# Column sums of the attention weights by GpSimd and a two-part bf16 product, with a new order of all steps

## The chip, the cores and the metric

The kernel runs on one core of a Trainium2 chip. The core has TensorE for matrix products (PE in the profile; PEld are its weight loads), VectorE (DVE), ScalarE (ACT) and GpSimd (POOL) for elementwise work, and SyncE (SP), whose queue issues DMA transfers here, as GpSimd's queue does too. The metric is the device time of one execution in microseconds (us). Three runs of the kernel before took 220.65, 221.41 and 221.46 us, the median is 221.41.

## The reference

Eight batches of eight heads, 512 tokens of 64 features and 32 state rows per head. Attention goes both ways between tokens and state; the result, 544 rows of 512 features per batch, goes through a layer of 2048 features with a periodic activation.

```
scores  = scale * x @ state.T          a  = softmax(scores)     xread = a @ state
scores2 = scale * state @ x.T          a2 = softmax(scores2)    sread = a2 @ x
y = concatenate([xread, sread], axis=tokens)        # heads side by side: 512 features
h = y @ w_in
g = h + sin(alpha * h)**2 / (alpha + 1e-9)
out = g @ w_out
```

Both softmaxes use the same exponentials E (tokens by state): `a` divides them by their sums over the state rows, `a2` by their sums over the tokens, which are the column sums of E.

## The kernel before, in words

The whole program is a list of steps by name, `ORDER`. The kernel walks through it; each step calls a method of `Steps`, and nothing is rescheduled: every engine executes its instructions in the order of the list and waits only for what it reads, for what it overwrites, and for a free buffer. A step's suffixes are its batch and tile numbers, the engine (A, V or G) and, where it opens one, a PSUM bank. There are eight banks of one tile each, so a step that opens a bank waits until the tile that held it has been read.

For a batch b the steps are:

- `lx` loads x (GpSimd's queue, cast to bf16), `pk` packs it by token, `td` transposes it by DMA (SyncE's queue). Batch 0 comes in by `lq`, `xq`, `xtq`, `xc` instead, and batch 1 is transposed on TensorE by `xt`, `xc`.
- `sc` makes the scores, `ex` the exponentials E (two groups of four heads), `rs` and `rr` their row sums and reciprocals (VectorE), `nm` the normalized A (GpSimd), `ad` its DMA transpose AT (SyncE's queue; `at`, `ac` for batch 0).
- `m` makes M, state times w_in, one slab of 512 columns at a time for both groups: eight matmuls of 64 x 32 tiles, that run side by side. `me` copies a slab out of PSUM, one group at a time. w_in arrives in four slices (`li`), one per slab, w_out in four (`lo`), one per four feature tiles, both from GpSimd's queue.
- `h` makes one feature tile of 128 columns for the 512 tokens, AT and M multiplied and summed over two groups (`hg` is one group's half of it). `si` is the sine (ScalarE), `sq` its square (on A, V or G by the suffix), `gt` puts g together on VectorE. The bank of h is read by `si` and by `gt`.
- `o` multiplies gT of a feature tile with w_out and adds it to one of four blocks of 128 tokens; `oc` copies a finished block out of PSUM and `os` stores it from SyncE's queue. There are six buffers for finished blocks.
- `w` multiplies E with x over four token blocks (16 matmuls of 64 columns), `cs` makes the column sums, `rc` their reciprocals, `xs` the normalized state rows. All eight batches' state rows go through the layer together as a ninth block, t = 8 (four products of 256 columns per feature tile).
- `warm_up` multiplies a tile of zeros, into a bank that nobody reads.

`cs` as it was: for each of four token blocks and each of two head parities r, ones (128 x 64) times 128 columns of E, into the upper or the lower half of the partitions; eight matmuls per batch, each on half of the array's columns.

Of the kernel before, what the change touches and what calls it, by code (L numbers as in the profile page):

```python
# [10 lines left out]
ALU = mybir.AluOpType  # L11
# [22 lines left out]
me.1.1.1.A warm_up.2.128.2 gt.0.2 si.0.0 warm_up.2.128.2 warm_up.2.128.6 warm_up.2.128.3
warm_up.2.128.2 warm_up.2.128.6 me.0.1.0.A gt.0.1 sq.0.0.G m.0.2.3.2 si.0.3 m.1.2.5.6 hg.0.4.0.7
me.0.2.0.V me.0.2.1.A hg.0.4.1 sq.0.3.G hg.0.6.0.4 me.1.2.1.V hg.0.6.1 si.0.4 hg.0.7.0.3 hg.0.11.0.2
me.1.2.0.V si.0.6 hg.0.7.1 sq.0.4.G hg.0.5.0.6 gt.0.0 hg.0.5.1 si.0.7 hg.0.11.1 hg.0.8.0.5 hg.0.8.1
sq.0.6.A gt.0.3 sq.0.7.G o.0.3.0.2.0 si.0.5 gt.0.4 o.0.3.2.3 o.0.0.0.2.1 si.0.11 o.0.0.2.3 gt.0.6
sq.0.5.G o.0.0.3.4 o.0.2.0.1.7 si.0.8 o.0.3.3.5 sq.0.11.A gt.0.7 hg.0.9.0.4 sq.0.8.G o.0.2.1.2
gt.0.5 o.0.2.2.4 hg.0.9.1 gt.0.11 o.0.0.4.5 hg.0.10.0.3 si.0.9 o.0.2.4.5 gt.0.8 o.0.0.5.6 o.0.3.5.6  # L40
sq.0.9.A o.0.3.6.8 pk.1.0.V hg.0.10.1 xt.1.1.6 pk.1.1.V si.0.10 gt.0.9 xt.1.0.2 xc.1.1.0.A sq.0.10.G
o.0.2.5.6 xc.1.1.1.V xc.1.0.0.A o.0.0.6.7 xc.1.0.1.V o.0.0.7.8 o.0.2.6.7 sc.1.1.5 gt.0.10 sc.1.0.4
m.0.3.6.2 ex.1.0 o.0.2.7.8 me.0.3.0.V o.0.1.0.3.3 me.0.3.1.V o.0.1.3.6 hg.0.13.0.6 o.0.1.6.7 ex.1.1
rs.1.0 hg.0.13.1 m.1.3.2.4 si.0.13 o.0.1.7.8 rr.1.0 rs.1.1 nm.1.0.0.4.G o.0.1.8.9 hg.0.12.0.5
o.0.3.8.9 rr.1.1 hg.0.12.1 me.1.3.0.V o.0.0.8.9 nm.1.1.0.4.G o.0.1.9.10 o.0.0.9.10 me.1.3.1.V
si.0.12 o.0.0.10.11 o.0.3.9.11 sq.0.13.G ad.1 hg.0.15.0.2 sq.0.12.A o.0.1.10.12 hg.0.15.1 gt.0.12
o.0.2.8.10 si.0.15 o.0.2.10.11 gt.0.13 o.0.0.11.12 hg.0.14.0.4 sq.0.15.A hg.0.14.1 o.0.3.11.13
si.0.14 gt.0.15 o.0.0.12.13 o.0.1.12.13 o.0.3.13.14 sq.0.14.A pk.2.0.V o.0.1.13.14 pk.2.1.V h.1.2.5
gt.0.14 h.1.4.6 td.2 si.1.2 lx.3.0.1 h.1.0.2 si.1.4 o.0.0.13.15 sq.1.2.V h.1.1.4 si.1.0 gt.1.2
sq.1.4.G o.0.3.14.16 si.1.1 o.0.2.11.13 sq.1.0.A oc.0.3.V h.1.6.5 sq.1.1.G gt.1.4 o.0.2.13.14 os.0.3  # L50
h.1.3.0 si.1.6 gt.1.0 o.0.1.14.16 si.1.3 sq.1.6.G h.1.13.6 gt.1.1 oc.0.1.A o.0.2.14.15 o.0.0.15.16
si.1.13 h.1.15.2 sq.1.3.G lx.4.0.1 gt.1.6 os.0.1 o.0.2.15.16 oc.0.0.A h.1.5.4 sq.1.13.V oc.0.2.V
si.1.15 h.1.7.3 os.0.0 gt.1.3 o.1.1.0.1.5 si.1.5 os.0.2 h.1.8.1 sq.1.15.G gt.1.13 o.1.1.1.2 si.1.7
o.1.2.0.2.7 sq.1.5.A o.1.1.2.3 sq.1.7.G h.1.12.0 gt.1.15 si.1.8 h.1.9.6 gt.1.5 o.1.2.2.3 si.1.12
sq.1.8.G o.1.2.3.5 gt.1.7 si.1.9 o.1.1.3.4 h.1.10.2 sq.1.12.A pk.3.1.V h.1.11.4 sq.1.9.G gt.1.8
o.1.2.5.6 si.1.10 o.1.2.6.7 gt.1.12 h.1.14.3 si.1.11 sq.1.10.G o.1.2.7.8 gt.1.9 sc.2.1.1 si.1.14
o.1.1.4.7 sq.1.11.A pk.3.0.V sq.1.14.G o.1.1.7.8 gt.1.10 td.3 o.1.2.8.9 sc.2.0.0 o.1.1.8.9 gt.1.11
o.1.1.9.10 ex.2.0 o.1.3.0.2.6 gt.1.14 o.1.3.2.4 o.1.2.9.10 o.1.3.4.5 o.1.2.10.12 ex.2.1 o.1.2.12.13
rs.2.0 o.1.1.10.11 m.2.2.2.4.3.0 rr.2.0 rs.2.1 o.1.2.13.14 nm.2.0.0.4.G me.2.3.0.A o.1.2.14.15 w.0.1
rr.2.1 me.2.2.1.A me.2.3.1.V o.1.3.5.6 nm.2.1.0.4.G me.2.2.0.A o.1.3.6.7 o.1.2.15.16 cs.0 oc.1.2.A  # L60
m.2.0.3.4.0.2 ad.2 rc.0 o.1.3.7.8 me.2.1.1.A o.1.3.8.9 sc.3.0.7 xs.0.1 me.2.1.0.A o.1.1.11.12 os.1.2
me.2.0.0.V sc.3.1.2 me.2.0.1.A o.1.1.12.13 o.1.3.9.10 xs.0.0 pk.4.1.V pk.4.0.V td.4 o.1.3.10.11
ex.3.0 o.1.1.13.16 ex.3.1 rs.3.0 o.1.3.11.13 oc.1.1.A o.1.3.13.14 rr.3.0 h.2.0.0 rs.3.1 nm.3.0.0.4.G
os.1.1 o.1.3.14.16 si.2.0 rr.3.1 h.2.1.3 oc.1.3.V nm.3.1.0.4.G h.2.2.4 h.2.8.1 os.1.3 h.2.3.7 ad.3
si.2.2 o.1.0.0.3.2 si.2.8 sq.2.0.V o.1.0.3.4 sq.2.2.G gt.2.0 h.2.4.5 si.2.1 o.1.0.4.6 si.2.3
sq.2.8.G o.1.0.6.7 gt.2.2 h.2.9.6 si.2.4 o.2.3.0.1.0 o.1.0.7.8 sq.2.1.G o.1.0.8.9 sq.2.3.A gt.2.8
o.1.0.9.10 h.2.5.4 si.2.9 gt.2.3 o.1.0.10.11 sq.2.4.G o.1.0.11.12 si.2.5 h.2.7.1 gt.2.1 o.1.0.12.13
sq.2.9.A sq.2.5.G o.1.0.13.14 gt.2.4 o.1.0.14.15 si.2.7 o.1.0.15.16 o.2.0.0.1.7 gt.2.9 o.2.0.1.2
oc.1.0.A h.2.6.3 sq.2.7.G gt.2.5 o.2.3.1.2 os.1.0 o.2.3.2.3 si.2.6 h.2.10.5 o.2.3.3.4 sq.2.6.A
# [88 lines left out]
class Steps:  # L158
# [505 lines left out]
```

## Time and profile before

| what | value |
|---|---|
| median of three runs | 221.41 us |
| the profiled execution | 221.22 us |
| its span, first to last instruction | 219.2 us |
| granted TensorE clock | 1.00 |
| VectorE: gT (L576) | 96.8 us in 144 |
| VectorE: squares (L201) | 7.0 us in 16 |
| ScalarE: Sin (L560) | 88.8 us in 144 |
| ScalarE: squares (L569) | 31.4 us in 53 |
| GpSimd: squares (L201) | 75.9 us in 75 |
| GpSimd: A (L201) | 16.6 us in 16 |

"Busy" is the time in which an engine executes; overlapping instructions count once. For each group of instructions the profile shows the line, the engine, the tiles written and read, the number, the busy time, the mean duration of one and the idle time ahead of them with what ended it. A matmul's duration includes the time that its result takes to come out, which overlaps with the next one; the chain of waits shows the distance from one to the next, so costs on TensorE are read from it. "issue" is time for which the profile shows no wait.

### The profile page before, as it was taken

How to read it: one execution, taken by the hardware profiler on the slowest of the kernel's cores; microseconds unless marked ns; L12 is line 12 of the kernel's file. 1: busy time of each engine (PE TensorE's matmuls, PEld its weight loads, DVE VectorE, ACT ScalarE, POOL GpSimd, SP SyncE). 2: the span in 40 equal slices, each digit the busy share in tenths (PEclk: the TensorE clock that was granted, in tenths of full speed). 3: DMA queues.
4: the chain of work that ended last, by engine and by line, in shares of the span. 5: the costliest groups of instructions: out<-in, count | busy, mean ns of one | idle time of the engine just before them, and what ended most of it. 6: DMA issues, size and time to landing. Idle time of an engine off the chain costs nothing.

```text
span 219.2 us, 4303 instructions
## 1 busy us (share of the span) xinstructions
PE 211.4 (96%) x1593; PEld 104.5 (48%) x1619; DVE 162.9 (74%) x287; ACT 173.4 (79%) x297; POOL 106.2 (48%) x114
## 2 busy tenths in 40 slices
PE   7989999999999999999999999999999999999994
PEld 3744544444444534444454444454445555665452
DVE  3769996999787789989888788888667987661201
ACT  4799778997998979898996999798848896785111
POOL 5959533895195647753943387273501082121000
PEclk9999999999999999999999999999999999999999
DMA  6999999987491029167145327470220211012042
GB/s 195 178 206 204 205 204 146 217 169 133 101 238 48 3 92 143 57 144 96 48 79 131 109 71 96 134 110 0 48 100 0 98 48 48 0 51 96 1 143 96
DMA packets 38052, 23.48 MB, mean 107 GB/s; under 512 B 20992, under 2 KB 33680, under 8 KB 38032
## 3 DMA queue, kind: packets, MB, share of 16 engines
q1 hardware_dynamic: 26128, 15.08, 26.5%
q0 software_dynamic: 11648, 8.13, 26.0%
q8 instruction: 12, 0.20, 0.3%
q14 instruction: 8, 0.07, 0.1%
q10 hardware_dynamic: 256, 0.01, 0.1%
HBM read 17.44 MB, written 8.91 MB: 120 GB/s over the span
## 4 chain that ended last, share of the span: by engine, by line
PE 90%; DMA 6%; POOL 1%; issue 1%; ACT 0%
PE o_ps L587 54%; PE h_ps L537 22%; DMA w_in_sb<-in_moe_w_in_dram 5%; PE m_ps L488 4%; PE h_ps L543 3%; PE h_ps L552 2%; PE w_ps L450 2%; PE s_ps L399 2%; PE w_ps L461 1%; DMA s<-in_state_dram 1%; POOL w_in_sb L282 1%; PE x_ps L376 0%; POOL st_nat L267 0%; POOL s01b L255 0%; ACT o_sb L595 0%
## 5 line engine op out<-in xcount | busy, mean ns | idle before, releaser
L587 PE MATMUL o_ps<-w_out_sb,gT 128*128 128x512 bf16 (+2 forms) x542 | 133.9, 373 | 1.6 <-issue 1.0
L576 DVE SCALAR_TENSOR_TENSOR gT<-s,inva_sb,h_ps 128x512 bf16<-128x512 bf16 (+1 forms) x144 | 96.8, 713 | 20.4 <-POOL s L201 10.8
L201 POOL TENSOR_TENSOR s<-s 128x512 bf16<-128x512 bf16 (+1 forms) x75 | 75.9, 1022 | 64.4 <-ACT s L560 62.7
L560 ACT ACTIVATE s<-h_ps,alpha_sb 128x512 bf16<-128x512 f32 (+1 forms) x144 | 88.8, 670 | 11.1 <-PE h_ps L543 4.5
L587 PEld LDWEIGHTS <-gT 128*128 128x128 bf16 x560 | 52.3, 98 | 60.3 <-issue 5.0
L537 PE MATMUL h_ps<-AT,M 128*128 128x512 bf16 x219 | 60.0, 379 | 0.3
L537 PEld LDWEIGHTS <-M 128*128 128x128 bf16 x224 | 21.7, 98 | 25.9 <-issue 0.4
L569 ACT ACTIVATE s<-s 128x512 bf16<-128x512 bf16 (+1 forms) x53 | 31.4, 594 | 0.8
L201 POOL TENSOR_TENSOR A<-E,rR 128x512 bf16<-128x512 bf16 x16 | 16.6, 1056 | 23.8 <-ACT o_sb L595 12.9
L595 ACT COPY o_sb<-o_ps 128x512 f32<-128x512 f32 (+2 forms) x24 | 13.7, 570 | 16.6 <-PE o_ps L587 16.5
L496 ACT CAST M<-m_ps 128x512 bf16<-128x512 f32 x35 | 18.6, 594 | 8.2 <-PE m_ps L488 8.2
L496 DVE CAST M<-m_ps 128x512 bf16<-128x512 f32 x29 | 18.9, 679 | 2.5 <-PE m_ps L488 2.1
L595 DVE COPY o_sb<-o_ps 128x512 f32<-128x512 f32 x11 | 7.5, 685 | 12.9 <-PE o_ps L587 12.9
L201 DVE TENSOR_TENSOR s<-s 128x512 bf16<-128x512 bf16 (+1 forms) x16 | 7.0, 439 | 6.2 <-ACT s L560 6.1
L410 DVE TENSOR_REDUCE R<-E 128x16 f32<-128x512 bf16 x16 | 10.4, 657 | 0.7 <-ACT E L406 0.6
L488 PE MATMUL m_ps<-w_in_sb,stT 64*32 64x512 bf16 x256 | 10.2, 382 | 0.1
L468 DVE RECIPROCAL rC<-w_ps 128x128 f32<-128x128 f32 x8 | 7.6, 948 | 3.3 <-PE w_ps L461 3.2
L303 PE MATMUL warm_ps<-warm 128*128 128x128 bf16 (+3 forms) x66 | 8.6, 271 | 1.4 <-DVE warm L209 1.2
L552 PE MATMUL h_ps<-AT,M 128*128 128x512 bf16 x29 | 8.4, 379 | 0.9 <-ACT M L496 0.7
L406 ACT ACTIVATE E<-s_ps 128x512 bf16<-128x512 f32 x16 | 8.8, 602 | 0.4 <-PE s_ps L399 0.4
L543 PE MATMUL h_ps<-xs_all,w_in_sb 128*128 128x256 bf16 x64 | 9.1, 273 | 0.0
L543 PEld LDWEIGHTS <-w_in_sb 128*128 128x128 bf16 x64 | 6.3, 98 | 3.4
(56 smaller groups left out, 101.8 us busy)
## 6 DMA issues: line engine op xcount, KB each, us to landing
out_dram<-o_sb SPq DMA_DIRECT2D x33, 256.0 KB, 2.3
xnat<-in_x_dram POOLq DMA_DIRECT2D x7, 512.0 KB, 7.5
w_in_sb<-in_moe_w_in_dram POOLq DMA_DIRECT2D x4, 512.0 KB, 10.9
w_out_sb<-in_moe_w_out_dram POOLq DMA_DIRECT2D x4, 512.0 KB, 18.0
x<-in_x_dram SPq DMA_DIRECT2D x4, 256.0 KB, 4.2
st_nat<-in_state_dram POOLq DMA_DIRECT2D x1, 256.0 KB, 5.3
out_dram<-o_sb SPq DMA_DIRECT2D x1, 192.0 KB, 1.9
s<-in_state_dram SPq DMA_DIRECT2D x1, 128.0 KB, 2.2
```

Source lines behind the costliest of these rows:

```text
L201: {"V": k.nc.vector, "G": k.nc.gpsimd}[eng].tensor_tensor(out, a, b, ALU.mult)
L410: k.nc.vector.reduce_sum(R[:, g], k.t["E", b][:, g].rearrange("p c (h j) -> p (c h) j", j=k.Ns), axis=AX.X)
L488: k.nc.tensor.matmul(k.t["m", b, s + n, g][o0:o0 + k.Ns, :], k.stT[k.half(r), b * k.G + g, c0:c0 + k.Ns], k.w_in_sb[k.half(r), 2 * g + h, ...
L496: k.copy(eng)(k.t["M", b][:, g, s * k.FW:(s + 1) * k.FW], k.t["m", b, s, g][:])
L537: k.nc.tensor.matmul(hp[:, :n], k.t["M", t][:, g, fs], k.t["AT", t][:, g, :], start=(g == 0), stop=(g == k.G - 1),)
L543: k.nc.tensor.matmul(hp[:, :n], k.w_in_sb[:, q, fs], k.xs_all[:, q].rearrange("p b j -> p (b j)"), start=(q == 0), stop=(q == k.Q - 1),)
L552: k.nc.tensor.matmul(k.t["h", t, f][:], k.t["M", t][:, g, f * k.P:(f + 1) * k.P], k.t["AT", t][:, g, :], start=(g == 0), stop=(g == k.G - 1),)
L560: k.nc.scalar.activation(s[:, :n], k.t["h", t, f][:, :n], ACT.Sin, scale=k.alpha_sb[:, f:f + 1])
L569: k.nc.scalar.activation(s2[:, :n], s[:, :n], ACT.Square)
L576: k.nc.vector.scalar_tensor_tensor(gT[:, :n], k.t["s2", t, f][:, :n], k.inva_sb[:, f:f + 1], k.t["h", t, f][:, :n], ALU.mult, ALU.add,)
L587: k.nc.tensor.matmul(k.t["o", t, st, half][:, cols], k.t["gT", t, f][:, rows], k.w_out_sb[:, f, cols], start=(f == 0), stop=(f == k.FT - 1),)
L595: k.copy(eng)(o_sb[:, cols], k.t["o", t, st, half][:, cols])
```

## The change

The column sums are made another way. GpSimd first adds the four token blocks of E in fp32: `ca` adds blocks 0 and 1 to blocks 2 and 3 (512 sums per partition), `cb` adds the two halves (256). `ch` rounds the result to bf16 and `cl` subtracts the rounded part from the fp32 sum and rounds the rest, so that two bf16 tiles hold the sum. `w` then has four more matmuls per batch (parity r, part p) in place of `cs`'s eight: 128 columns each, with `sel`, a tile of 64 columns of zeros, 64 of ones and 64 of zeros, of which a window of 128 columns puts the sums into one half of the partitions and adds nothing to the other.

```diff
-        k.ones = const.tile([P, k.D], BF16, name="ones")
+        k.sump, k.hlp = pool("sump", 1), pool("hlp", 2)
+        k.sel = const.tile([P, 3 * k.D], BF16, name="sel")
...
+    def ca(k, b):
+        k.t["sum", b] = k.sump.tile([k.P, 2, k.G, k.P], FP32, name="sum")
+        E = k.t["E", b][:].rearrange("p g i c -> p i g c")
+        k.nc.gpsimd.tensor_tensor(k.t["sum", b][:], E[:, 0:2], E[:, 2:4], ALU.add)
+
+    def cb(k, b):
+        t = k.t["sum", b]
+        k.nc.gpsimd.tensor_tensor(t[:, 0], t[:, 0], t[:, 1], ALU.add)
+
+    def ch(k, b):
+        hl = k.new(b, "hilo", k.hlp, [k.P, 2, k.G, k.P], BF16)
+        k.nc.gpsimd.tensor_copy(hl[:, 0], k.t["sum", b][:, 0])
+
+    def cl(k, b):
+        hl = k.t["hilo", b]
+        k.nc.gpsimd.tensor_tensor(hl[:, 1], k.t["sum", b][:, 0], hl[:, 0], ALU.subtract)
+
     def w(k, b, bank):
...
-    def cs(k, b):
-        E, wc = k.t["E", b], k.t["w", b]
-        for i in range(k.C):
-            for r in range(2):
-                Ev = E[:, :, i, :].rearrange("p g (h r j) -> p g h r j", h=2, r=2)
+        for r in range(2):
+            for p in range(2):
+                Ev = k.t["hilo", b][:, p].rearrange("p g (h r j) -> p g h r j", h=2, r=2)
                 k.nc.tensor.matmul(
-                    wc[k.half(r), :, 2 * k.Ns:], k.ones[:], Ev[:, :, :, r],
-                    start=(i == 0), stop=(i == k.C - 1),
+                    wc[:, :, 2 * k.Ns:], k.sel[:, (1 - r) * k.D:(3 - r) * k.D], Ev[:, :, :, r],
+                    start=(r == 0 and p == 0), stop=(r == 1 and p == 1),
                 )
```

The list of steps is new from end to end. `o` and `hg` now stand for one matmul each, and the first one that is issued starts the sum in the bank (`oo` and `ho` only open the bank), so that feature tiles and groups come in any order; `m` makes one slab per step.

```diff
+    def ho(k, t, f, bank):
+        k.t["h", t, f] = k.ps(bank, [k.P, k.S], FP32, "h_ps")
+        k.made["h", t, f] = 0
+
+    def oo(k, t, st, bank, half=None):
+        k.t["o", t, st, half] = k.ps(bank, [k.P, k.DOUT], FP32, "o_ps")
+        k.made["o", t, st, half] = 0
+
-    def o(k, t, st, f0, f1, *bank, half=None):
+    def o(k, t, st, f, half=None):
...
+            start=k.made["o", t, st, half] == 1, stop=k.made["o", t, st, half] == k.FT,
```

Some stretches of the list, before and after, around the steps that the prediction speaks of (start; block 3 and 4; block 5; end):

```diff
-ac.0.0.V m.0.0.6.4 m.1.0.1.2 lo.3 at.0.1.7 me.0.0.0.V me.0.0.1.A warm_up.2.128.0 warm_up.2.128.3
-me.1.0.1.A ac.0.1.V hg.0.2.0.5 me.1.0.0.V hg.0.1.0.4 hg.0.2.1 hg.0.1.1 hg.0.0.0.0 lx.2.0.1 si.0.2
-hg.0.0.1 m.1.1.6.3 si.0.1 m.0.1.7.2 hg.0.3.0.1 me.0.1.1.A sq.0.2.V hg.0.3.1 sq.0.1.G me.1.1.0.V
-me.1.1.1.A warm_up.2.128.2 gt.0.2 si.0.0 warm_up.2.128.2 warm_up.2.128.6 warm_up.2.128.3
-warm_up.2.128.2 warm_up.2.128.6 me.0.1.0.A gt.0.1 sq.0.0.G m.0.2.3.2 si.0.3 m.1.2.5.6 hg.0.4.0.7
-me.0.2.0.V me.0.2.1.A hg.0.4.1 sq.0.3.G hg.0.6.0.4 me.1.2.1.V hg.0.6.1 si.0.4 hg.0.7.0.3 hg.0.11.0.2
-me.1.2.0.V si.0.6 hg.0.7.1 sq.0.4.G hg.0.5.0.6 gt.0.0 hg.0.5.1 si.0.7 hg.0.11.1 hg.0.8.0.5 hg.0.8.1
-sq.0.6.A gt.0.3 sq.0.7.G o.0.3.0.2.0 si.0.5 gt.0.4 o.0.3.2.3 o.0.0.0.2.1 si.0.11 o.0.0.2.3 gt.0.6
+m.1.0.0.6 me.1.0.0.A nm.0.1.0.4.G at.0.1.4 ac.0.1.V lo.3 ho.0.3.7 hg.0.3.0 al_c inva hg.0.3.1 si.0.3
+me.1.0.1.V lx.2.0.1 sq.0.3.V hg.0.1.0 hg.0.1.1 ho.0.2.0 hg.0.2.1 m.0.1.2.4 me.0.1.1.V si.0.1
+sq.0.1.V me.0.1.0.A hg.0.2.0 si.0.2 sq.0.2.G ho.0.0.6 m.1.1.5.1 me.1.1.0.A hg.0.0.0 hg.0.0.1
+ho.0.6.4 hg.0.6.1 gt.0.3 si.0.0 sq.0.0.G hg.0.6.0 me.1.1.1.A ho.0.5.2 hg.0.5.0 gt.0.1 hg.0.5.1
+m.0.2.7.5 me.0.2.1.A gt.0.2 ho.0.7.3 hg.0.7.1 me.0.2.0.V ho.0.4.1 hg.0.4.1 hg.0.7.0 m.1.2.0.5 si.0.6
+sq.0.6.G gt.0.0 me.1.2.1.A me.1.2.0.V hg.0.4.0 si.0.4 gt.0.6 sq.0.4.V gt.0.4 ho.0.10.7 hg.0.10.0
+si.0.5 sq.0.5.G si.0.7 sq.0.7.G hg.0.10.1 ho.0.9.5 hg.0.9.1 hg.0.9.0 gt.0.5 ho.0.11.6 hg.0.11.0
+oo.0.0.0 o.0.0.2 o.0.0.3 o.0.0.0 ca.0 cb.0 ch.0 hg.0.11.1 si.0.11 sq.0.11.V oo.0.3.4 o.0.3.1 o.0.3.3
...
+o.2.3.12 o.2.0.14 sq.2.0.G o.2.0.12 xs.1.1 o.2.3.9 m.3.0.4.3 m.3.1.0.7 o.2.1.2 ca.2 me.3.0.1.A cb.2
+ch.2 gt.2.0 me.3.0.0.V o.2.3.4 o.2.3.8 me.3.1.1.A o.2.0.0 sc.4.0.4 o.2.3.10 ex.4.0 o.2.1.8
+me.3.1.0.V m.3.3.0.7 m.3.2.3.6 rs.4.1 rr.4.1 h.3.0.4 o.2.3.0 o.2.0.5 me.3.3.0.V me.3.3.1.A o.2.0.1
+nm.4.1.0.4.G o.2.0.6 me.3.2.1.A cl.2 o.2.1.0 me.3.2.0.V oo.2.2.3 o.2.2.14 o.2.2.3 rs.4.0 rr.4.0
+si.3.0 h.3.12.6 si.3.12 nm.4.0.0.4.G o.2.3.2 h.3.8.0 o.2.0.7 h.3.9.7 oc.2.3.V sq.3.12.V gt.3.12
+os.2.3 lx.5.0.1 si.3.8 sq.3.8.V si.3.9 gt.3.8 sq.3.0.V gt.3.0 h.3.4.5 sq.3.9.G gt.3.9 o.2.2.1 si.3.4
+o.2.1.12 o.2.0.8 h.3.13.6 si.3.13 sq.3.13.A gt.3.13 o.2.1.9 o.2.2.7 sq.3.4.G o.2.2.6 os.1.2 gt.3.4
+ad.4 o.2.2.0 h.3.3.0 si.3.3 o.2.0.11 o.2.0.15 o.2.1.10 oc.2.0.A sq.3.3.G gt.3.3 h.3.11.4 o.2.1.7
+si.3.11 sq.3.11.G os.1.0 gt.3.11 o.2.1.3 o.2.2.5 oc.2.1.A os.2.1 h.3.7.1 si.3.7 sq.3.7.G o.2.2.8
+m.4.3.6.7 me.4.3.1.V m.4.2.2.5 me.4.2.0.A pk.5.0.V gt.3.7 o.2.2.11 me.4.2.1.A h.3.15.0 si.3.15
...
+oc.5.1.A os.4.1 o.6.3.9 xs.7.0 gt.7.6 xs.7.1 o.6.3.8 oo.6.1.7 o.6.1.0 o.6.1.7 h.6.13.2 o.6.1.1
+h.7.0.4 si.7.0 sq.7.0.V gt.7.0 cb.5 ch.5 o.6.1.2 o.6.2.4 cl.5 o.6.2.12 si.6.13 o.6.1.12 sq.6.13.G
+o.6.2.15 o.6.2.6 gt.6.13 o.6.2.10 h.7.5.3 si.7.5 sq.7.5.A w.5.1 rc.5 o.6.0.8 xs.5.1 o.6.3.6 o.6.2.11
+h.7.13.4 si.7.13 sq.7.13.G xs.5.0 os.5.3 gt.7.5 gt.7.13 o.6.2.7 o.6.1.4 h.7.10.2 o.6.0.12 si.7.10
+sq.7.10.A gt.7.10 o.6.0.13 o.6.3.10 h.8.14.1 si.8.14 o.6.2.0 o.6.3.4 sq.8.14.V gt.8.14 o.6.0.5
...
-oc.7.0.A o.7.2.2.5 os.7.0 o.7.2.5.11 oh.7.3.0.1 o.7.2.11.13 och.7.3.0.A o.7.2.13.15 osh.7.3.0
-o.7.2.15.16 oh.7.3.1.4 oc.7.2.V os.7.2 och.7.3.1.A osh.7.3.1
+oc.7.2.A os.7.2 o.7.1.3 o.7.0.9 o.7.1.11 o.7.1.13 o.7.1.8 o.7.1.10 oc.7.1.V o.8.0.14 o.8.0.12
+o.7.0.12 o.8.0.7 o.8.0.11 os.7.1 o.7.0.0 o.8.0.0 oc.8.0.V os.8.0 oh.7.3.0.4 o.7.0.3 o.7.0.4
+och.7.3.0.V osh.7.3.0 oh.7.3.1.7 och.7.3.1.A oc.7.0.V os.7.0 osh.7.3.1
```

What each engine has to do in the two lists:

| work | before | after |
|---|---|---|
| warm-up matmuls | 66 | 14 |
| column-sum matmuls | 64 on half of the array's columns | 32 on all of them |
| squares, 512 columns, on VectorE / ScalarE / GpSimd | 15 / 42 / 71 | 46 / 35 / 47 |
| squares, 256 columns, on VectorE / ScalarE / GpSimd | 1 / 11 / 4 | 5 / 3 / 8 |
| copies of M on VectorE / ScalarE | 29 / 35 | 27 / 37 |
| packs of batch 0 on VectorE / ScalarE | 0 / 4 | 3 / 1 |
| copies of stT of the later batches on VectorE / ScalarE | 1 / 3 | 2 / 2 |
| `ca`, `cb`, `ch`, `cl` on GpSimd | 0 | 8 each |

GpSimd's queue issues the loads in the same sequence as before; on SyncE's queue, `os` steps stand later among the transposes `td` and `ad` than they did.

## The prediction

> **What bounds the kernel now.** I read the page's busy shares first, then TensorE's waits, then the chain of work that ended last, then single stretches of the timeline.
>
> ```profile
> PE 211.4 (96%) x1593; PEld 104.5 (48%) x1619; DVE 162.9 (74%) x287; ACT 173.4 (79%) x297; POOL 106.2 (48%) x114
> ```
>
> TensorE is busy nearly all the time, but busy shares alone don't say that it is never late. Its waits, for the window from 17.4 us to the end, do:
>
> ```profile
> engine line waited for: us in total, times, longest us
> PE o_ps L587 <- issue: 1.0, 6, 0.2
> PE h_ps L552 <- issue: 0.2, 1, 0.2
> ```
>
> It waits for no other engine and no transfer there; the 1.2 us of "issue" are changes between tile shapes. What sets the start of that stretch is in the chain from 4 to 18 us:
>
> ```profile
> 4.11 1.47 POOL w_in_sb L282 x2
> 5.58 11.79 DMA w_in_sb<-in_moe_w_in_dram
> 17.37 0.04 issue
> 17.41 0.60 PE m_ps L488 x9
> ```
>
> The third slice of w_in, issued at 5.58 us, lands at 17.37, and the matmuls m.0.2 that read it start 0.04 us later. So the span is three pieces: 17.4 us up to that landing, 198.7 us of gapless matmuls up to 216.1 (the last stretch of the timeline starts at 205.77 and lasts 10.35), and 3.1 us for the last copy and store. Faster means less matmul work behind that landing, or more of it done ahead of it.
>
> **The change, part by part.** The profiled run took 221.22 us: a span of 219.2 and 2.0 around it. The median of the runs shown is 221.41, so I add 0.2 at the end.
>
> Column sums on TensorE. Chain rows, start, duration and work:
>
> ```profile
> 55.55 0.34 PE w_ps L461 x8
> 55.90 0.56 PE m_ps L488 x16
> ...
> 57.23 0.22 PE o_ps L587
> ```
>
> Eight narrow matmuls of one block take 0.34 us, eight blocks 2.6 (L461 has 1.2% of the chain). The new ones are four per block, 128 columns over the whole array. The nearest row:
>
> ```profile
> 9.90 1.62 PE L303 MATMUL warm_ps<-warm 128*128 128x128 bf16 x26
> ```
>
> The last of the 26 needs 0.22 us itself, so (1.62 - 0.22)/25 = 56 ns from one to the next, 32 x 56 ns = 1.8 us. Gain 0.84 us. Bounds: 0.8, and 1.2 if the change of tile shape ahead of the narrow ones (0.09 each, the difference between 0.56 and 0.47 where w meets the column sums) goes in four of the blocks.
>
> Work ahead of the landing. Before, eight hg matmuls (feature tiles 2, 1, 0, 3) stand ahead of m.0.2; now twelve (3, 1, 2, 0, 6, 5). Each takes 0.22 us on the chain (57.23 above is such a row), so 4 x 0.216 = 0.86 us moves into time that is spent waiting. It is really hidden only if they fit: m.0.1 starts when the second slice lands, 4.85 + 10.1 = 14.95 us; behind it stand eight hg and m.1.1, and the sum of their rows ends at 17.3, just under 17.41.
>
> m.0.2 and m.1.2, one pair before, now stand apart. A pair costs 0.56, a single 0.34 plus 0.09 of shape change in front of it: +0.22 us. Later slabs are still adjacent in pairs.
>
> First o product. From m.0.2 to it there are now 2.73 us of matmuls, so 20.14 at best. I followed ScalarE's queue by its rows (Sin three in 1.91 us when back to back, a copy of M 0.48 to 0.6): it has three Sin and five M copies between 15.4 and 19.6 and is never idle there, m.1.2 and hg.0.9.1 each wait about 0.1 us for an M copy to free their bank, and the first o product comes at 20.35. +0.2 us.
>
> Sum on TensorE: -0.84 - 0.86 + 0.22 + 0.2 = -1.28 us.
>
> GpSimd. It loses 24 squares of 512 columns (mean 1045 ns, 25.1 us) and gains 4 of 256 (612 ns, 2.4) and 32 fp32 steps. The trace has no fp32 sum. Lower bound, as bf16 of the same width: ca 1.05, cb 0.61, ch 0.40 (the cast of s01b, 396 ns, is the same shape and types), cl 0.61, 2.7 us per block. Upper bound: twice that for the three that read or write fp32, 4.9. I take 2.7: the one row with fp32 input, the cast, costs less for 256 columns than the bf16 product of 256 (396 against 612 ns). So 21 to 39 us added, GpSimd at 105 to 122 us of 219: not a bound. New wait: w's second half waits for cl, and everything behind it on TensorE with it. Adding up the matmuls between cl and w in the order gives 7.8 us or more for seven blocks, but 1.5 us for block 5; at the upper price w.5 is some 1 us late, and rc.5, xs.5 and the first h.8 behind it. Value 0, range to +1.
> For a 2048-element fp32 sum the Trainium skill (GPSIMD Engine Reference, section "3.1 Elementwise — side-by-side cycle accounting") states 4497 ns; scaled to ca's 512 and cb's and cl's 256 elements that is an estimate of 2.7 us per block with ch, the same sum. No run here shows it yet.
>
> VectorE. It gains 31 squares of 512 (449 ns) and 4 of 256 (285), three packs of x0 and one copy of stT, and loses two M copies: 13.9 + 1.1 + 2.4 (three packs as on ScalarE now, 618 ns, and 549) - 1.4 (679 each) = +16 us, 179 of 219. The mean hides the dense part: from m.3.0 to m.4.3 the order puts on VectorE nine gT (0.67 when back to back: five in 3.36 us), four M copies (0.63), three squares, two sums and two reciprocals of R and an o_sb copy, 12.3 us beside 11.5 us of matmuls. Before, no stretch of that length has over 1.04 times the matmul time by the same rows. And its squares can wait for GpSimd. Timeline, start and duration:
>
> ```profile
> 60.95 1.05 POOL L201 TENSOR_TENSOR A<-E,rR 128x512 bf16<-128x512 bf16 x1
> 60.97 0.75 PEld L537 LDWEIGHTS <-M 128*128 128x128 bf16 x4
> 61.02 1.42 SPq L602 DMA_DIRECT2D out_dram<-o_sb  x2
> 61.62 0.66 DVE L201 TENSOR_TENSOR s<-s 128x512 bf16<-128x512 bf16 x1 [0.41 <-ACT s L560]
> ```
>
> This square starts while GpSimd is at work until 62.00 and takes 0.66; alone it takes 0.42. So 0.24 us per meeting, up to 1.05 if it came right behind a GpSimd start. With GpSimd at work about half of the time and 46 squares, 46 x 0.5 x 0.24 = 5.5 us more on VectorE (before: 15 squares, 1.8). Hand-following the stretch at m.3, me.3.2.0.V ends about when o.2.2.14 needs its bank: wait 0 to 0.1. I take 0 for VectorE as a whole, because bank and gT slack elsewhere absorb a lag of a microsecond; without that cover it is the second rival.
> The Trainium skill speaks against this part (SBUF — State Buffer, section "🔬 SBUF: two separate sides"): a VectorE step with two SBUF inputs and a GpSimd step that reads SBUF hold a shared port exclusively, and the later one is blocked for the whole instruction. That agrees with the 0.66; by the rule alone the 46 squares would pay half a GpSimd step, 0.5 us, at each meeting, 12 us on VectorE, and the forecast would be that rival.
>
> Startup. Three packs of x0 go from ScalarE to VectorE, and warm-ups fall from 66 to 14. A's normalization waits for GpSimd's DMA issues (10.15 us), which are the same, so a pack that is 0.5 us late is covered. Fewer warm-ups may leave TensorE at half pace: its first seven 512-column matmuls are 0.43 us apart, later ones 0.22. Between 6.5 and 13.4 us the order still has some 4.7 us of matmuls by their rows, so I take 0; without that, eight hg cost twice, +1.7.
>
> ScalarE loses 15 squares (0.42 to 0.64) and gains two M copies: it only gets lighter. SyncE: stores are moved behind transposes and later stores (os.1.2 behind os.2.3), with oc.2.1 waiting for the buffer; landing takes 1.8 to 5.3 us, 0 to +1, value 0. The copy of the last 384-column piece goes to VectorE, with 1.3 us of matmuls behind it instead of 2.0, so its store starts 0.6 us nearer the end and may hold up the last one: 0 to +0.4, value 0.1.
>
> Sum: -1.28 + 0.1 = -1.2 us, 221.22 - 1.2 = 220.0, on the median's footing **220.2 us**.
>
> **The rivals.**
> - VectorE becomes the bound in blocks 3 and 4 and TensorE waits for gT and for banks. It decides once VectorE's work, waits included, exceeds the matmuls by more than the 1 us of slack. Place: m.3.0 to m.4.3, 12.3 + 3 x 0.24 + 3 x 0.24 for steps that GpSimd's fp32 stretches hold = 13.7 beside 11.5, and from gt.3.6 to the first reciprocal of block 5 (19 gT, six squares, three M copies, two packs at 0.38, two sums, rc at 0.95, two xs at 0.28, an o_sb copy and a reciprocal), 21.7 + 6 x 0.24 = 23.1 beside 20: 5.3 us over, less 1 us of slack in each and 0.6 us regained between, 2.7. Time 222.9, slower. For it: the rows above. Against it: gT is often needed only microseconds later, and no such wait is seen now at 1.04.
> - The clock or the start slips: TensorE is at half pace or ScalarE is late before 17.4, +1.2 to 1.7, 221.4 to 221.9, the gain undone. For it: the 17.3 against 17.41. Against it: warm-ups remain around every gap.
> - The order holds no stall at all and the narrow-tile gain is the full 1.2: 220.2 - 0.4 - 0.3 = 219.5.
>
> **How the numbers follow.** Forecast 0.55, VectorE bound 0.25, slipped start 0.12, no stall 0.08. The forecast's own range is 219.6 to 221.0. About 0.5% of 221.41, 1.1 us, is what a measurement here can tell from no change: the line lies at 220.3, just above the forecast. Faster by more: 0.38 of the forecast's 0.55 and the 0.08, 0.46. Slower (over 222.5): the 0.25, and 0.03 of mixtures, 0.28. Within: 0.26. Range: 219.2 (no stall and all bounds good) to 222.9 (VectorE).
>
> **What would show it.** Right: m.0.2 again at 17.4, twelve hg ahead of it, the first o product near 20.35, TensorE's waits after that under 0.5 us, L480 at 0.22 us per block, cl well ahead of w. Wrong: TensorE idle before gT, M or o_sb in blocks 3 and 4; squares on VectorE with a mean over 600 ns; GpSimd's fp32 sums at 2 us; 0.43 us between matmuls beyond 8 us; a wait of h.8 for xs.

## The result and the profile after

The changed kernel takes 223.34 us (median of six runs, 222.45 to 224.26) against 221.30 us of the kernel before in the same comparison: a ratio of 1.010, 95% interval 1.007 to 1.013. It is slower by about 2 us; the forecast was 220.2 us. The profiled execution of the changed kernel took 224.26 us, so it is the slowest of the six and shows about 0.9 us more than the median. The few executions of any kernel that ran markedly slower than its others, one of them profiled at a granted clock of 0.56, are left out of the ratios and readings below.

The busy row of its page first:

```profile
PE 210.7 (95%) x1507; PEld 101.1 (46%) x1535; DVE 179.3 (81%) x325; ACT 167.8 (76%) x280; POOL 109.9 (49%) x126
```

VectorE went from 162.9 to 179.3 us (the forecast said 179), GpSimd from 106.2 to 109.9, and TensorE is busy for a little less time in a longer span. So TensorE waits more. Its waits from 17.4 us to the end, where the view of before has only 1.2 us of "issue" (what waited, for what, us in total, times, longest):

```profile
PE h_ps L556 <- DMA AT<-A: 1.9, 1, 1.9
PE m_ps L507 <- DMA w_in_sb<-in_moe_w_in_dram: 0.9, 1, 0.9
PE o_ps L611 <- issue: 0.6, 4, 0.2
PE o_ps L611 <- DVE gT L598: 0.6, 1, 0.6
```

Two more of 0.2 us are left out. Two of those shown are new: a wait for a transposition of A, and one for gT. The wait for w_in's third slice is not new; before, warm-ups filled the time up to 17.41. Now the twelve hg products are done at 17.09 us, and TensorE stands until the slice has landed at 17.95. The chain of waits over the largest of them (start, duration, what):

```profile
84.00 0.70 DVE o_sb L619
...
84.72 0.33 SPq L626
...
85.11 0.42 SPq L626
...
85.70 8.62 DMA AT<-A
94.31 0.14 issue
94.45 1.46 PE h_ps L556 x6
```

Read from below: the first h of block 4 starts at 94.45, when AT has landed; its transposition was issued at 85.70 by SyncE and took 8.62 us; SyncE was busy with two stores (L626) before it, and these waited for an o_sb copy by VectorE. GpSimd had finished A itself at 84.47. Beside it on the DMA engines (tile, issuer, KB each, us from issue to landing), first in the changed kernel, then in the kernel before, same window of 78 to 97 us:

```profile
out_dram<-o_sb SPq DMA_DIRECT2D x4, 256.0 KB, 5.7
xnat<-in_x_dram POOLq DMA_DIRECT2D x1, 512.0 KB, 9.4
AT<-A SPq DMA_TRANSPOSE x1, 8.6
```

```profile
out_dram<-o_sb SPq DMA_DIRECT2D x4, 256.0 KB, 2.3
xnat<-in_x_dram POOLq DMA_DIRECT2D x1, 512.0 KB, 7.5
AT<-A SPq DMA_TRANSPOSE x1, 6.7
```

The transposition was slow before too. But there it was issued at 81.59 and first read at about 95.2, 13.6 us later; now TensorE could read it at 92.4, 6.7 us after its issue. SyncE's row of before:

```profile
81.59 1.24 SPq L440 DMA_TRANSPOSE AT<-A  x1
```

Where the 3.0 us between the two profiled spans lie, from the start of m.0.2 and the end of the last matmul in the two timelines:

| piece | before | after |
|---|---|---|
| start of m.0.2 | 17.41 | 17.99 |
| m.0.2 to the last matmul | 198.71 | 200.85 |
| last matmul to the end of the span | 3.09 | 3.35 |

### The profile page after: what moved, and what is told of

Read it like the earlier page. It is cut to its first block, busy times and chain, and to the rows that moved or that the text cites. A ratio compares the mean times of both kernels' runs of the same rounds, so it can differ in the third digit from the quotient of the medians.

```text
span 222.2 us, 4123 instructions
## 1 busy us (share of the span) xinstructions
PE 210.7 (95%) x1507; PEld 101.1 (46%) x1535; DVE 179.3 (81%) x325; ACT 167.8 (76%) x280; POOL 109.9 (49%) x126
## 4 chain that ended last, share of the span: by engine, by line
PE 79%; DMA 10%; DVE 3%; ACT 2%; POOL 2%; issue 1%; SPq 0%; ACTq 0%
PE o_ps L611 47%; PE h_ps L556 20%; DMA w_in_sb<-in_moe_w_in_dram 6%; DMA AT<-A 4%; PE m_ps L507 3%; PE h_ps L562 3%; DVE gT L598 2%; PE w_ps L472 2%; PE s_ps L404 1%; DMA s<-in_state_dram 1%; ACT M L515 1%; DVE s L205 1%; ACT s L582 1%; PE h_ps L574 1%; PE w_ps L480 1%
## 5 line engine op out<-in xcount | busy, mean ns | idle before, releaser
L598 DVE SCALAR_TENSOR_TENSOR gT<-s,inva_sb,h_ps 128x512 bf16<-128x512 bf16 (+1 forms) x144 | 98.7, 714 | 13.4 <-POOL s L205 8.2
L205 POOL TENSOR_TENSOR s<-s 128x512 bf16<-128x512 bf16 (+1 forms) x55 | 55.2, 1011 | 69.2 <-ACT s L582 68.5
L556 PE MATMUL h_ps<-AT,M 128*128 128x512 bf16 x218 | 61.3, 379 | 2.5 <-DMA AT<-A 1.9
L205 DVE TENSOR_TENSOR s<-s 128x512 bf16<-128x512 bf16 (+1 forms) x51 | 23.2, 455 | 6.1 <-ACT s L582 5.5
L515 ACT CAST M<-m_ps 128x512 bf16<-128x512 f32 x37 | 20.2, 592 | 8.5 <-PE m_ps L507 8.4
L591 ACT ACTIVATE s<-s 128x512 bf16<-128x512 bf16 (+1 forms) x38 | 23.2, 613 | 1.0
L619 ACT COPY o_sb<-o_ps 128x512 f32<-128x512 f32 (+1 forms) x24 | 13.8, 576 | 13.0 <-PE o_ps L611 13.0
L619 DVE COPY o_sb<-o_ps 128x512 f32<-128x512 f32 (+1 forms) x11 | 7.3, 674 | 6.9 <-PE o_ps L611 6.8
L453 POOL TENSOR_TENSOR sum<-E 128x512 f32<-128x512 bf16 x8 | 9.4, 1175 | 0.2
L574 PE MATMUL h_ps<-AT,M 128*128 128x512 bf16 x30 | 8.7, 381 | 0.3 <-DVE M L515 0.3
L353 DVE COPY xp<-xnat 128x1024 bf16<-128x1024 bf16 x14 | 7.0, 510 | 1.5 <-DMA xnat<-in_x_dram 1.5
```

Of the source, the lines that this page charges most:

```text
L205: {"V": k.nc.vector, "G": k.nc.gpsimd}[eng].tensor_tensor(out, a, b, ALU.mult)
L515: k.copy(eng)(k.t["M", b][:, g, s * k.FW:(s + 1) * k.FW], k.t["m", b, s, g][:])
L556: k.nc.tensor.matmul(hp[:, :n], k.t["M", t][:, g, fs], k.t["AT", t][:, g, :], start=(g == 0), stop=(g == k.G - 1),)
L574: k.nc.tensor.matmul(k.t["h", t, f][:], k.t["M", t][:, g, f * k.P:(f + 1) * k.P], k.t["AT", t][:, g, :], start=k.made["h", t, f] == 1, sto ...
L591: k.nc.scalar.activation(s2[:, :n], s[:, :n], ACT.Square)
L598: k.nc.vector.scalar_tensor_tensor(gT[:, :n], k.t["s2", t, f][:, :n], k.inva_sb[:, f:f + 1], k.t["h", t, f][:, :n], ALU.mult, ALU.add,)
```

## The experiments

Every kernel was run beside the kernel before, 6 to 12 executions each; a ratio is to the kernel before of the same comparison.

### The transposition's place, and the load's

Theory: SyncE's order made the transposition late. Rival: the load of x for block 5, issued by GpSimd 1.3 us before it. One kernel moves the one, one the other.

```diff
-si.3.0 h.3.12.6 si.3.12 nm.4.0.0.4.G o.2.3.2
+si.3.0 h.3.12.6 si.3.12 nm.4.0.0.4.G ad.4 o.2.3.2
...
-ad.4 o.2.2.0 h.3.3.0
+o.2.2.0 h.3.3.0
```

> The changed kernel with one step moved: the transposition of A of block 4 (line 445) stands on SyncE's queue directly behind the GpSimd step that makes A, ahead of the two stores of lines 626 that it stood behind. Theory (SyncE's order makes the transposition late): it is issued about 1.2 us earlier (84.5 instead of 85.70) and the two stores no longer share the DMA engines with it, so AT lands by about 89, TensorE's wait of 1.9 us before h of block 4 at 92.5 is gone, and the time falls by about 2 us to 221.3 us. Rival (it is late because the 512 KB load of x, issued at 84.4, shares the DMA engines): AT still lands some 8 us after its issue, at 92 to 93, the wait shrinks by 1.2 us at most, and the time is 222.2 us or more. Second rival (VectorE is behind in blocks 3 and 4 anyway): the wait moves to gT, and the time stays within 0.5 us of 223.3.

```diff
-o.2.3.12 o.2.0.14 sq.2.0.G
+o.2.3.12 o.2.0.14 lx.5.0.1 sq.2.0.G
...
-os.2.3 lx.5.0.1 si.3.8
+os.2.3 si.3.8
```

> The changed kernel with one step moved: GpSimd issues the 512 KB load of x for block 5 (line 280) about 10 us earlier, ahead of its last square of block 2, so that it is over before the transposition of A of block 4 is issued; SyncE's order stays. Theory (SyncE's order): the transposition is still issued at 85.7 behind the two stores, and most of the wait stays: time 222.5 us or more. Rival (the load shares the DMA engines): the transposition takes 3 to 4 us in place of 8.6, lands by 89.5, and the wait of 1.9 us is gone: about 221.3 us.

The transposition first: 222.62 us (221.92 to 223.76), ratio 1.0055 (1.0035 to 1.0076). The load earlier: 221.34 us (220.16 to 221.99), ratio 0.9989 (0.9969 to 1.0009). So the load is the larger cause: moving it gives 2.0 us, and SyncE's order alone is worth 0.7. The DMA rows of the two, transposition first above, load earlier below:

```profile
xnat<-in_x_dram POOLq DMA_DIRECT2D x1, 512.0 KB, 9.3
AT<-A SPq DMA_TRANSPOSE x1, 8.1
```

```profile
out_dram<-o_sb SPq DMA_DIRECT2D x4, 256.0 KB, 2.3
xnat<-in_x_dram POOLq DMA_DIRECT2D x1, 512.0 KB, 5.9
AT<-A SPq DMA_TRANSPOSE x1, 3.2
```

Issued at 84.04, 0.09 us behind the load, the transposition still took 8.1 us. With the load gone it took 3.2 although two stores stood in front of it on SyncE. And in the first kernel the load took over as the end of the chain; from 84 to 96 us it reads:

```profile
83.95 9.25 DMA xnat<-in_x_dram
93.21 0.02 issue
93.23 0.43 DVE xp L353
93.66 0.66 DVE gT L598
94.31 0.53 DVE s L205
```

The load itself takes 9.25 instead of 5.9 us, VectorE stands at the pack of block 5 (L353) until it lands, and gT is queued behind the pack. That is a second harm of the same meeting, which the wait for AT had covered.

Does the load still matter when it comes behind the transposition? In the next kernel the transposition is first on SyncE, the load comes one GpSimd square later, and the first pack stands beside the second so as not to wait.

```diff
-nm.4.0.0.4.G o.2.3.2
+nm.4.0.0.4.G ad.4 o.2.3.2
...
-os.2.3 lx.5.0.1 si.3.8 sq.3.8.V si.3.9 gt.3.8 sq.3.0.V gt.3.0 h.3.4.5 sq.3.9.G
+os.2.3 si.3.8 sq.3.8.V si.3.9 gt.3.8 sq.3.0.V gt.3.0 h.3.4.5 sq.3.9.G lx.5.0.1
...
-me.4.2.0.A pk.5.0.V gt.3.7
+me.4.2.0.A gt.3.7
...
-si.3.6 pk.5.1.V
+si.3.6 pk.5.0.V pk.5.1.V
```

> The changed kernel with the transposition of A of block 4 directly behind its maker on SyncE's queue (issued at about 84.0), the load of x for block 5 issued by GpSimd one square later (about 85.5, so behind the transposition and not 0.1 us ahead of it), and VectorE's first pack of block 5 put beside its second, so that it doesn't wait for the later load. If the order in which the two enter the DMA engines decides: AT lands about 3 to 4 us after its issue, by 88, no stall at 92, and the time is near that with the load moved ahead, 221.3 us. If the two share the engines whatever the order: AT takes 6 to 8 us, lands at 90 to 92, just before TensorE wants it, and the time is 221.3 to 222 us with a wait of less than 0.5 us; the landing tells these apart, not the time.

```profile
xnat<-in_x_dram POOLq DMA_DIRECT2D x1, 512.0 KB, 8.0
AT<-A SPq DMA_TRANSPOSE x1, 3.1
```

The transposition, issued at 83.75, landed in 3.1 us; the load, issued at 86.49, took 8.0. So a load issued 2.7 us behind the transposition does it no harm, and no wait for AT is left. By then the transposition had only 0.36 us to go, so this run doesn't show what would happen with the two issued side by side, transposition first. The time, 221.91 us (ratio 1.0021, 0.9996 to 1.0046), is 0.6 over the kernel with the load moved, with intervals that overlap; its profile has the wait for gT near 22 us that is treated below.

On queues the Trainium skill (DMA: Bandwidth & Descriptors, section "🔬 Queues, rings and completion order") says that each DMA engine goes round between the queues that have work, a packet at a time. The traces show where the slow transposition spends its time. These are the packets of the kernel with the transposition 0.09 us behind the load, from 84 to 87.7 us and from 87.7 to 88.9 (queue, packets, MB, share of the 16 engines, in which packets can overlap; q1 is SyncE's queue, q0 GpSimd's with the load):

```profile
q1 hardware_dynamic: 1024, 0.26, 42.0%
q0 software_dynamic: 177, 0.09, 24.7%
```

```profile
q0 software_dynamic: 287, 0.15, 105.7%
```

The 1024 small packets are the transposition. They moved from 85.2 to 87.6, the load's from 86.7 on; with the load moved they took 1.4 us (85.6 to 87.1). But the landing was reported at 92.1, 4.5 us after the last of them, while the load's packets went on; with the load moved it was 0.5 us after. In the kernel before, the packets were through at 85.6 and the landing came at 88.25. Only in the changed kernel, with two stores and the load ahead, were the packets themselves late: nearly all moved from 89.8 on, 4.1 us after the issue. Taking turns would stretch the moving of the packets; in two of the three cases most of the lost time lies between the last packet and the landing, so it does not account for it. Why the landing is told so late, and why the packets start so late in the changed kernel, no run shows.

Last, the kernel before with the load moved ahead in the same way, to see whether its slow transposition cost anything:

> The kernel before with the load of x for block 5 issued some 10 us earlier, between GpSimd's squares of block 2. There the transposition of A of block 4 took 6.7 us beside that load, with some 11 us between its issue and its first use. If that time was hidden: the transposition falls to 3 to 4 us, and the time stays within 0.2 us of 221.4. If the load or the transposition cost something there too: 0.3 us or more below.

The transposition fell from 6.7 to 3.1 us, and the time stayed: 221.58 us, ratio 1.0015 (0.9992 to 1.0037); from m.0.2 to the last matmul it takes 198.74 us, before 198.71. So 6.7 us were free with 13.6 us of cover (the "some 11" of the expectation is too low), and 8.6 cost 2 us with 6.7.

### The column sums

The changed kernel with the old sums, and the kernel before with the new ones (there with the four GpSimd steps of a block side by side, and four buffers for their result instead of two; one block is shown). Where the expectations say 16 products for each block, it is eight:

```diff
-oo.0.0.0 o.0.0.2 o.0.0.3 o.0.0.0 ca.0 cb.0 ch.0 hg.0.11.1
+oo.0.0.0 o.0.0.2 o.0.0.3 o.0.0.0 hg.0.11.1
...
-o.1.0.11 w.0.7 ad.2
+o.1.0.11 w.0.7 cs.0 ad.2
```

> The changed kernel in its own order, but with the column sums made by TensorE as in the kernel before (16 products for each block behind the w products) and the four GpSimd steps of each block left out. If the new sums save what their matmuls say (0.84 us by the prediction's sum, 1.2 us by the counts), this is 0.8 to 1.2 us slower than the changed kernel: 224.1 to 224.5 us. Rival (the four GpSimd steps delay VectorE by the shared lock and GpSimd's own squares by more than they bring): it is as fast as the changed kernel or faster, 223.3 us or less.

```diff
-gt.1.2 sq.1.4.G
+gt.1.2 ca.0 cb.0 ch.0 cl.0 sq.1.4.G
...
-o.1.2.15.16 cs.0 oc.1.2.A
+o.1.2.15.16 oc.1.2.A
```

> The kernel before in its own order, with the new column sums alone: 16 products for each block leave TensorE, the four GpSimd steps stand in idle stretches of GpSimd, the w products take the two bf16 parts. If the sums are a gain and the new order is what lost: 220.1 to 220.6 us, 0.8 to 1.2 us under the kernel before. Rival (the GpSimd steps hold VectorE or late squares and cost what they bring): 221.2 us or more.

> The kernel before in its own order with the new column sums alone, once more, as the measure for the run beside it: 219.9 to 220.6 us, 0.4 to 0.8% under the kernel before.

Old sums in the changed order: 224.45 us, ratio 1.0139 (1.0107 to 1.0172), 0.4% over the changed kernel's 1.010. New sums in the old order: 220.28 us, ratio 0.994 (0.9917 to 0.9963), and once more 219.85 us, ratio 0.993 (0.9916 to 0.9944). That is 1.2 and 1.5 us under the kernel before, and it is the fastest kernel here. One block in the timelines (start, us, line, tiles, shape), before above, the new sums in the old order below:

```profile
76.11 0.63 PE L450 MATMUL w_ps<-E,xp 128*128 128x64 bf16 x16
76.67 0.41 PE L461 MATMUL w_ps<-E,ones 128*64 128x128 bf16 x8
77.02 0.61 PE L587 MATMUL o_ps<-w_out_sb,gT 128*128 128x512 bf16 x2
```

```profile
76.39 0.63 PE L470 MATMUL w_ps<-E,xp 128*128 128x64 bf16 x16
76.85 0.39 PE L478 MATMUL w_ps<-hilo,sel 128*128 128x128 bf16 x4
77.08 0.59 PE L604 MATMUL o_ps<-w_out_sb,gT 128*128 128x512 bf16 x2
```

From the first w product to the next o product 0.91 us before and 0.69 now. The four new matmuls take the 4 x 56 ns of the forecast; the eight old ones cost 0.44, of which 0.09 is the change to half-width tiles in front of them. Two blocks of before have their old sums side by side:

```profile
170.14 0.64 PE L461 MATMUL w_ps<-E,ones 128*64 128x128 bf16 x16
170.71 0.39 PE L537 MATMUL h_ps<-AT,M 128*128 128x512 bf16 x1
```

Sixteen last 0.57 us to the next product where eight last 0.35, so eight more cost 0.22, as much as the four new ones. The products themselves are no cheaper: what the new sums save is the changes of tile shape, 0.09 us into the narrow tiles and 0.12 out of them.

### A square that meets GpSimd's

In the profile of the changed kernel two o products at 22.63 are 0.98 us apart, where 0.216 is usual: 0.76 us lost to a wait for gT (0.6 in the view of waits). What VectorE and GpSimd did ahead of it, one row of each; first the changed kernel, then the kernel with the load moved, which has no such wait:

```profile
21.45 1.04 POOL L205 TENSOR_TENSOR s<-s 128x512 bf16<-128x512 bf16 x1 [0.66 <-ACT s L582]
...
21.49 1.28 DVE L205 TENSOR_TENSOR s<-s 128x512 bf16<-128x512 bf16 x1
```

```profile
21.10 2.30 POOL L205 TENSOR_TENSOR s<-s 128x512 bf16<-128x512 bf16 x2 [0.72 <-ACT s L582]
...
21.09 0.42 DVE L205 TENSOR_TENSOR s<-s 128x512 bf16<-128x512 bf16 x1
```

GpSimd 0.04 us ahead: VectorE's square takes 1.28 us instead of 0.42, the gT behind it comes 0.86 us later, and TensorE waits for gT. VectorE 0.01 us ahead: its square takes 0.42 and GpSimd's first of the two 1.30. The two programs are the same up to here. Of the seven profiles with this square on VectorE (granted clock near 1), four have GpSimd ahead by 0.04 us, 1.28 us and the wait; three have VectorE level or ahead by 0.01, 0.42 us and no wait. In the four, TensorE had stood for 0.4 to 1.0 us directly ahead of m.0.2, in the three for 0.3 at most. So how the start went may be what decides; no run tests it. That the one that starts first keeps the other out is what the Trainium skill states (SBUF — State Buffer, section "🔬 SBUF: two separate sides"), and here the rows agree. Three runs put this square on ScalarE, one in the changed kernel and two with the load moved; a fourth is the measure for the last of them:

```diff
-si.0.4 gt.0.6 sq.0.4.V gt.0.4
+si.0.4 gt.0.6 sq.0.4.A gt.0.4
```

> The changed kernel with one square moved: the fifth square of block 0 (line 205, before gT of that block) goes from VectorE to ScalarE. In the profile of the changed kernel it took 1.28 us on VectorE, between two squares of GpSimd, and TensorE then stood 0.76 us before an o product at 22.6; but with the load of block 5 moved the same square took 0.42 us and the stall was not there. Theory (VectorE held by GpSimd's squares in some executions): the median falls by 0.3 to 0.7 us, to 222.6 to 223.0. Rival (ScalarE's queue takes the wait over, as the forecast had it for the first o product): 223.2 us or more.

> The changed kernel with both moves: the load of x for block 5 issued ahead of GpSimd's last square of block 2, and the fifth square of block 0 on ScalarE. If the two losses are separate and add up: 2.0 us and 0.3 to 0.7 us less than the changed kernel, 220.6 to 221.0 us. If the square is worth nothing: 221.3 us, as with the load alone.

> The changed kernel with the load of x for block 5 issued earlier and the fifth square of block 0 on ScalarE, once more, beside the kernel with the load alone. If that square's wait for GpSimd is what is left: 0.4 to 0.8 us under the run beside it, about 220.7 us. If it is worth nothing in the median: the same within 0.3 us.

> The changed kernel with the load of x for block 5 issued earlier, once more, as the measure for the run beside it: 221.1 to 221.6 us. In the profile, the square of block 0 on VectorE takes 1.28 us where it starts just behind GpSimd's, with a stall of TensorE of some 0.75 us near 22 us, or 0.42 us where it starts just ahead of it, with no stall; m.0.2 to the last matmul then takes about 198.9 or 197.9 us.

In the changed kernel alone the move gave nothing that can be told: 223.54 us, ratio 1.010 (1.006 to 1.014). With the load moved: 220.77 and 220.82 us with the square on ScalarE, 221.34 and 221.42 without. The ratios, 0.9987 and 0.9991 against 0.9989 and 0.9996, overlap widely. The executions put together, 24 with the move and 23 without, have medians of 220.79 and 221.39; 16 of the 24 took less than 221.0 us and 6 of the 23. That points to 0.6 us in the typical execution, but the line at 221.0 was drawn after the runs, so the gain in time is likely and not shown; what is shown is the wait in the profiles with the meeting and its absence in those without. The two profiled executions without the move had VectorE ahead by 0.01 us, and both were among the quick ones (220.73 and 220.49 us).

### The order by itself

Two kernels ask what the order was worth. The first is the changed order with the old sums and the load moved:

> The changed kernel's order without the new column sums (TensorE makes them as before, the four GpSimd steps are left out) and with the load of x for block 5 issued ahead of GpSimd's last square of block 2: what the order alone is worth without the late transposition. If it is worth what the forecast gave it (four hg products 0.86 us, less 0.5 us for m.0.2 and m.1.2 apart, the first o product and the tail): 221.0 us, 0.2% under the kernel before. If the small waits of the changed order (some 1 us in the profile) take that back and more: 222.2 to 222.6 us, 0.3 to 0.6% over the kernel before.

222.28 us, ratio 1.0044 (1.0028 to 1.0061): without the late transposition and without the new sums, the order is still 0.9 us slower than the one it replaced, not 0.3 us faster, as the prediction's terms for it make it (-0.86 + 0.22 + 0.2 + 0.1). Its profiled execution, the slowest of the eight, has the meeting above, with the 0.6 us wait for gT, so part of the 0.9 us is that meeting.

The second puts two more hg products ahead of m.0.2 in the old order, with the new sums:

```diff
-sq.0.1.G me.1.1.0.V
-me.1.1.1.A warm_up.2.128.2 gt.0.2 si.0.0 warm_up.2.128.2 warm_up.2.128.6 warm_up.2.128.3
-warm_up.2.128.2 warm_up.2.128.6 me.0.1.0.A gt.0.1 sq.0.0.G m.0.2.3.2 si.0.3 m.1.2.5.6 hg.0.4.0.7
-me.0.2.0.V me.0.2.1.A hg.0.4.1
+sq.0.1.G me.0.1.0.V me.1.1.1.A hg.0.4.0.7 hg.0.4.1 me.1.1.0.V gt.0.2 si.0.0 gt.0.1 sq.0.0.G
+m.0.2.3.2 si.0.3 m.1.2.5.6 me.0.2.0.V me.0.2.1.A
```

> The kernel before in its own order with the new column sums, and one thing from the changed order: the two hg products of one further column block (line 577 of the changed kernel's helper for h of block 0) stand ahead of the product m.0.2, in the place of twelve warm-up matmuls of 128 columns; to have their M in time, VectorE makes its copy and the copy of m.1.1 comes after. The forecast priced four such products at 0.86 us, so two are 0.43 us. Theory (they run in time in which TensorE only waits for slice 3 of w_in, and the saving stays): 0.43 us under the kernel with the sums alone, 219.6 to 220.0 us. Rival (VectorE's later copies and gT make small waits behind them, as in the changed order): 220.2 us or more.

220.55 us, ratio 0.9959 (0.9946 to 0.9972), against 219.85 us beside it: 0.7 us slower, not 0.4 us faster. Its waits of TensorE from 16.8 us on, where the kernel without the move has none:

```profile
PE m_ps L504 <- DVE gT L592: 0.3, 1, 0.3
PE h_ps L568 <- DVE gT L592: 0.2, 1, 0.2
```

m.1.2 now waits for gT to free its bank, because VectorE makes a copy of M first. TensorE's work was moved into idle time, and the queue behind it paid.

From m.0.2 to the last matmul, where the start and the tail play no part, the timelines give 197.57 us with the new sums in the old order, both times; 197.87 in the changed order with the load moved, 197.91 with the square moved too, 198.95 with the meeting (the transposition first, the load behind it). So the changed order has four hg products less in this stretch, 0.86 us of work, and is not shorter. The 1.2 us that this makes (0.86 and the 0.34 by which 197.91 is over 197.57) can be found from start to start in the two timelines. A 512-column product follows the last one after 0.216 us where nothing holds it. With both moves, four come 0.09 to 0.28 us later than that behind another one (0.63 in all), and three a few hundredths; in the old order with the new sums none does. m.0.2 and m.1.2 apart cost 0.24, the transposes of x of block 1 on TensorE 0.21, and two pairs of m start 0.11 late together. Most of these pieces are too small to appear in the view of waits.

## Why the prediction was wrong

The step that failed first is the term for SyncE: "stores are moved behind transposes and later stores (os.1.2 behind os.2.3) ... 0 to +1, value 0". It priced the landing of the stores. What was late was the transposition ad.4 in that queue: 1.2 us by the two stores ahead of it, and some 5 us by the load of x that GpSimd issues at 84.4; TensorE lost 2.1 us to it (its next product could have come at 92.37 and came at 94.45). The trace of before held the price, a transposition of 6.7 us among others of 3, but it was hidden there, and I did not ask how much cover the new order leaves it. Shown by three runs: the load moved (2.0 us gained), the load moved behind the transposition (3.1 us to landing), the kernel before with the load moved (no change). That the measured 223.3 us lies near the 222.9 of the rival in which VectorE bounds blocks 3 and 4 is chance: that rival's waits are not there.

Point by point:

- Column sums on TensorE, -0.84: right in kind, too small. Measured 1.2 and 1.5 us in the old order, 1.14 from m.0.2 to the last matmul in the profiles. Mis-sized: the change of shape in front, which the sum left out and only the bound of 1.2 had. Seven groups paid it (two blocks share one), 0.65 us; in four places where m stood behind the old sums, m now pays such a change itself, 0.37 in all. 0.84 + 0.65 - 0.37 is 1.1 us.
- Work ahead of the landing, -0.86: the twelve hg products did fit (TensorE was idle from 17.09 us). That the saving reaches the end is not borne out, and this is the second step that failed: small waits of 1.2 us behind them take it back, the order by itself is 0.9 us slower, and a pair of hg products alone lost 0.7.
- First o product: 2.92 us from m.0.2 to it, forecast 2.94. m.0.2 itself started 0.58 us later with its slice. That is a matter of the execution: the same start-up steps landed that slice anywhere from 17.16 to 18.20 us in nine profiles. The five of the old order have 16.53 to 17.37, so a delay of a few tenths by the new order isn't ruled out.
- VectorE, 0: its total was right (179), and so was the rejection of the rival in blocks 3 and 4: with the load moved the view shows no wait of TensorE there. The squares took 473 ns in the mean, far from 600. But one meeting in the start, where there is no slack, cost 0.76 us in the profile (the medians above differ by 0.6, which is not clear of the noise). I priced a mean meeting (0.24) and let slack absorb it; the price is that of the one meeting with a waiting reader.
- GpSimd, value 0: right. Its four steps take 3.07 us per block (2.7 by the prediction's rows and by its estimate from the page cited there, so both were 12% low):

```profile
L453 POOL TENSOR_TENSOR sum<-E 128x512 f32<-128x512 bf16 x8 | 9.4, 1175 | 0.2
...
L457 POOL TENSOR_TENSOR sum<-sum 128x256 f32<-128x256 f32 x8 | 6.0, 755 | 0.4
L465 POOL TENSOR_TENSOR hilo<-sum,hilo 128x256 bf16<-128x256 f32 x8 | 5.5, 684 | 0.6
...
L461 POOL CAST hilo<-sum 128x256 bf16<-128x256 f32 x8 | 3.6, 455 | 0.5
```

- The slipped start as a rival: fewer warm-ups cost nothing that the profile shows; from 13.6 us on the hg products are 0.22 us apart where nothing holds them.
- The reading of "issue", 1.2 us, as changes of tile shape was wrong, without effect on the sum: the kernel before with only the load moved has the same changes and no such rows from its m.0.2 on. At such a row the timeline of before is one product short (11 hg products behind m.0.2, where the list has twelve), so these rows are most likely missing records and not idle time.
- The tail, +0.1: 0.25 us (3.09 to 3.35).

In all, by the profiles: sums -1.14 (m.0.2 to the last matmul falls from 198.71 to 197.57 in the old order, and from 200.06 to 198.95 in the changed one, both with the meeting and without the late transposition), transposition +1.90 (200.85 against 198.95, both with the meeting), the execution with the meeting +1.08 (198.95 against 197.87, of which 0.76 at the one wait), the rest of the order +0.30 (197.87 against 197.57), the later slice +0.58, tail +0.25. That is 2.97 of the 2.98 us between the two spans.

What stays open: with both moves the changed kernel is at 220.8 us, 0.5 to 1.0 us over the new sums in the old order by medians. The profiles account for 0.6: 0.34 between m.0.2 and the last matmul and 0.27 in the tail. No run removed the small waits one by one. The load was moved only for block 5; whether another place for it does still better was not tried.

## What to carry to other kernels

When an order changes, list for every transfer the time from issue to first use in the old and the new order, and take its duration from its worst row, not its median: a slow transfer with cover shows no wait, and costs its full lateness when the cover is cut. Where a small transposition and a large load become ready together, issue the load when the transposition has all but landed (2.7 us later here), or early enough to have landed itself; 0.09 us apart helped little. A part of a change that is clearly good (here the sums) should be measured in the old order too, since it may be the whole of the gain.

## What the runs showed of the hardware

- The transposition of A of block 4 (256 KB) lands in 3.1 to 3.2 us without a 512 KB load beside it or with the load issued 2.7 us behind it, and in 6.7 to 8.7 us when the load was issued 0.1 to 1.3 us ahead of it, on another engine's queue. In two of the traces its packets were through 2.7 and 4.5 us before its landing was reported. The load takes 5.8 to 5.9 us with nothing beside it and 7.5 to 9.4 beside the transposition, the stores or both; stores of 256 KB go from 2.3 to 5.7 us.
- Eight column-sum products on 128 x 64 tiles and four on 128 x 128 take the same 0.22 us in a stream; the changes of tile shape cost 0.09 us in and 0.12 out.
- Of two squares on VectorE and GpSimd that start within 0.04 us of each other, the later one is held: VectorE takes 1.28 us against 0.42, ending 0.28 us behind GpSimd's (as in the prediction's row of 0.66 us), or GpSimd 1.30 against 1.04. Which one it is changes from run to run, and with it a wait of 0.76 us on TensorE.
- fp32 sums on GpSimd are only a little dearer than bf16 products of the same width: 1175 ns against 1079 for 512 columns (755 against 612 for 256).
